# Splitting the stores of the last two chunks into a multiple of 16 rows and a rest, and giving the last two token tiles their own PSUM banks and a second store queue

## Chip, cores, metric

One core of one Trainium2 chip runs the kernel. The metric is the device time of one execution in microseconds; lower is better. Beside the time there is a profile of an execution, whose span (first to last instruction) is about 1.8 us shorter than the time of the same execution.

Engines: PE is TensorE's matmul, ACT is ScalarE, DVE is VectorE, POOL is GpSimd, SP is the sync engine, which here only issues DMAs. A "store" is a DMA from SBUF to the output in HBM.

## The reference

```
X = rfft(x, axis=1);  Y = X * (filt_r + 1j*filt_i);  y = irfft(Y, n=3008)      # x: 8 x 3008 x 256
h = y.reshape(24064, 256) @ w_in                                                # 256 x 2048
g = h + sin(alpha*h)**2 / (alpha + 1e-9)
out = g @ w_out                                                                 # 24064 x 256, fp32
```

## The kernel before

The Fourier part runs interleaved with the two big products. The tokens are worked through in 48 chunks of 512 (some of 384) columns, counted from 0, so that chunk 47 is the last. For each chunk `hidden` computes the 2048 hidden values, and one chunk later `project` multiplies them with `w_out`, 128 tokens (one token tile) at a time. Columns stand in the order (n2, row), with 94 rows to an n2, so 128 consecutive columns hit two or three runs of output tokens, and each run is one store with one 1 KB row of the output per partition.

```python
C, NR, S, B = 256, 94, 3008, 8
chunks = [(pb, c0, 384 if c0 == 2560 else 512) for pb in range(B // 2)
          for c0 in [*range(0, 2561, 512), *range(2944, 2 * S, 512)]]

def project(k, u):
    pb, c0, n = chunks[k]
    t, half = divmod(u, 2)
    if t % 2 == 0 and half == 0:
        pso[k] = ops.tile([128, 2, C], FP32, name=f"po_{k}_{t}", tag="o")   # two tiles in one PSUM bank
    for jb in range(8 * half, 8 * half + 8):
        nc.tensor.matmul(out=pso[k][:, t % 2, :], lhsT=v[k][:, jb, 128 * t:128 * t + 128],
                         rhs=w2[:, jb, :], start=(jb == 0), stop=(jb == 15))
    last = 128 * (t + 1) == n
    if half == 1 and (t % 2 == 1 or last):
        nb = t % 2 + 1
        o = opool.tile([128, 2, C], FP32, name=f"o_{k}_{t}", tag="o")
        nc.scalar.copy(out=o[:, 0:nb, :], in_=pso[k][:, 0:nb, :])
        for i in range(nb):
            store(o[:, i, :], pb, c0 + 128 * (t + 1 - nb + i))

def store(o_blk, pb, col):
    p = 0
    while p < 128:
        odd, rest = divmod(col + p, S)
        n2, row = divmod(rest, NR)
        cnt = min(128 - p, NR - row)
        t0 = (2 * pb + odd) * S + 32 * row + n2
        nc.sync.dma_start(out=bass.AP(tensor=out.tensor, offset=out.offset + t0 * C,
                                      ap=[[32 * C, cnt], [1, C]]),
                          in_=o_blk[p:p + cnt, :])
        p += cnt
# ... (cut: transforms, tables, hidden, the schedule)
```

In the last chunk the four tiles (0 to 3) have stores of 42 and 86 rows; 8, 94 and 26; 68 and 60; 34 and 94. After the last `hidden` there is nothing but `project`, 128 matmuls in a row.

The Fourier part of batch 1 is loaded by POOL from an intermediate in HBM.

```python
def load_t2(self, g):
    self.t2[g] = t2pool.tile([128, 6, C], FP16, name=f"t2_{self.b}_{g}", tag="t2")
    for p in range(2):
        a0 = p * NS + 6 * g
        nc.gpsimd.dma_start(out=self.t2[g][64 * p:64 * p + 64, :, :],
                            in_=self.d1[a0:a0 + 6, :, :].rearrange("s n c -> n s c"))
```

Of the kernel before, what the change touches and what calls it, by code (L numbers as in the profile page):

```python
# [17 lines left out]
B, S, C = 8, 3008, 256  # L18
# [8 lines left out]
def dft_tables():  # L27

    n1, n2 = np.arange(N1), np.arange(N2)
    s, q = np.arange(NS), np.arange(NQ)  # L30
    ph = 2 * np.pi * np.outer(n1, s) / N1
    w = np.stack([np.cos(ph), -np.sin(ph)], 1)
    wf = np.zeros((N1, 2, 2, NS, 2))
    wi = np.zeros((2, NS, 2, N1, 2))
    v = np.stack([2 * np.cos(ph), -2 * np.sin(ph)], 0)
    v[0, :, 0], v[1, :, 0] = 1.0, 0.0
    for h in range(2):
        wf[:, h, :, :, h] = w
        wi[:, :, h, :, h] = v.transpose(0, 2, 1) * (8.0 / S)


    kap = np.where(q[:, None] < 32, s + N1 * q[:, None], s + N1 * (95 - q[:, None]))
    sg = np.where(q < 32, 1.0, -1.0)[:, None]
    th = 2 * np.pi * n2[:, None, None] * kap / S
    c, sn = np.cos(th), np.sin(th)
    d = np.zeros((2, N2, NS, 2, NQ))
    d[0, :, :, 0] = c.transpose(0, 2, 1)
    d[1, :, :, 0] = sn.transpose(0, 2, 1)
    d[0, :, :, 1] = (-sn * sg).transpose(0, 2, 1)
    d[1, :, :, 1] = (c * sg).transpose(0, 2, 1)  # L50
    f16 = np.float16
    wf, wi = wf.reshape(N1 * 2, 2, NS, 2), 2 * wi.reshape(2, NS, 2, NR)
    wf0, wi0 = np.zeros((NR, 2, 2, 32)), np.zeros((2, 2, 32, NR))
    wf0[:, :, :, :NS] = wf.transpose(0, 1, 3, 2)
    wi0[:, :, :NS] = wi.transpose(0, 2, 1, 3)
    return (wf.reshape(NR, NK).astype(f16), wi.reshape(NK, NR).astype(f16),
            d.reshape(128, NS, 128).astype(f16),
            wf0.reshape(NR, 128).astype(f16), wi0.reshape(128, NR).astype(f16))
# [3 lines left out]
def kernel(  # L62
# [9 lines left out]
):  # L72
    nc = tc.nc
    wf_host, wi_host, d_host, wf0_host, wi0_host = dft_tables()
    wf_dram = nc.inline_tensor(wf_host, name="wf_tbl")
    wi_dram = nc.inline_tensor(wi_host, name="wi_tbl")
# [13 lines left out]
    def pool(name, bufs, space=None):  # L90
        kw = {} if space is None else {"space": space}
        return ctx.enter_context(tc.tile_pool(name=name, bufs=bufs, **kw))
# [11 lines left out]
    fps = pool("fps", 2, PSUM)  # L104
    hps = pool("hps", 4, PSUM)
    ops = pool("ops", 2, PSUM)


    wf0_t = cpool.tile([NR, 128], FP16)
    nc.sync.dma_start(out=wf0_t, in_=wf0_dram.ap())  # L110
# [138 lines left out]
                                     lhsT=t4_h[ch // 2][0:NK, n0 % 16 + i, cb * 128:cb * 128 + 128])  # L249
            evac(y[:, cb, self.b % 2, n0:n0 + 4, :], psv, on_act)  # L250


    y = cpool.tile([128, 2, 2, 32, NR], FP16)
    y_cols = y.rearrange("p a b n r -> p a (b n r)")


    warm = cpool.tile([128, 1], FP32)
    nc.vector.memset(warm, 0.0)
# [11 lines left out]
    for g in range(2):  # L270
        for k, filt in enumerate((filt_r, filt_i)):
            for q in range(2):
                off, step = ((12 * g) * C, C) if q == 0 else ((N1 - 12 * g) * C, -C)
                marks["filt", g] = nc.gpsimd.dma_start(
                    out=f_t[k][64 * k + 32 * q:64 * k + 32 * q + 32, 12 * g:12 * g + 12, :],
                    in_=bass.AP(tensor=filt.tensor, offset=filt.offset + off,
                                ap=[[N1 * C, 32], [step, 12], [1, C]]))
# [59 lines left out]
    for i in range(4):  # L337
        turn(t2_0[i // 2][:, :, 32 * (i % 2):32 * (i % 2) + 32], t1_0[:, :, 32 * i:32 * i + 32])
        if i % 2 == 1:
            k = i // 2  # L340
            nc.vector.tensor_copy(out=f_t[k][64 - 64 * k:128 - 64 * k, 0:12, :],
                                  in_=f_t[k][64 * k:64 * k + 64, 0:12, :])
# [37 lines left out]
    for i in range(4):  # L380
        ins = nc.sync.dma_start(out=cos_all[:, i, :], in_=bass.AP(tensor=moe_alpha.tensor,
                                                                  offset=moe_alpha.offset + 512 * i,
                                                                  ap=[[0, 128], [1, 512]]))
# [54 lines left out]
    def weights_out(i):  # L438

        for jb in range(4 * i, 4 * i + 4):  # L440
            if jb in range(8, 16):
                nc.scalar.mul(w2[:, jb, :], w_out32[:, jb, :], rec_t[:, jb:jb + 1])  # L442
            else:
# [3 lines left out]
    chunks = [(pb, c0, 384 if c0 == 2560 else 512) for pb in range(B // 2)  # L447
              for c0 in [*range(0, 2561, 512), *range(2944, 2 * S, 512)]]

    v = {}  # L450
    pso = {}
# [16 lines left out]
    def project(k, u):  # L468

        pb, c0, n = chunks[k]  # L470
        t, half = divmod(u, 2)
        if t % 2 == 0 and half == 0:
            pso[k] = ops.tile([128, 2, C], FP32, name=f"po_{k}_{t}", tag="o")
        for jb in range(8 * half, 8 * half + 8):
            nc.tensor.matmul(out=pso[k][:, t % 2, :], lhsT=v[k][:, jb, 128 * t:128 * t + 128],  # L475
                             rhs=w2[:, jb, :], start=(jb == 0), stop=(jb == 15))
        last = 128 * (t + 1) == n
        if half == 1 and (t % 2 == 1 or last):
            nb = t % 2 + 1
            o = opool.tile([128, 2, C], FP32, name=f"o_{k}_{t}", tag="o")  # L480
            nc.scalar.copy(out=o[:, 0:nb, :], in_=pso[k][:, 0:nb, :])  # L481
            for i in range(nb):
                store(o[:, i, :], pb, c0 + 128 * (t + 1 - nb + i))

    def store(o_blk, pb, col):

        p = 0
        while p < 128:
            odd, rest = divmod(col + p, S)
            n2, row = divmod(rest, NR)  # L490
            cnt = min(128 - p, NR - row)
            t0 = (2 * pb + odd) * S + 32 * row + n2
            nc.sync.dma_start(  # L493
                out=bass.AP(tensor=out.tensor, offset=out.offset + t0 * C,
                            ap=[[32 * C, cnt], [1, C]]),
                in_=o_blk[p:p + cnt, :])
            p += cnt




    pending = []

# [52 lines left out]
    for k in range(len(chunks) + 1):  # L556
        for j in range(8):
            if k < len(chunks):
                hidden(k, 2 * j)
                hidden(k, 2 * j + 1)  # L560
            slot(step)
            if k > 0:
                n_half = 2 * (chunks[k - 1][2] // 128)
                for u in range(n_half * j // 8, n_half * (j + 1) // 8):
                    project(k - 1, u)
            slot(step + 0.5)
            step += 1
# [31 lines left out]
```

## Time and profile before

| | before |
|---|---|
| time, median of 3 runs | 809.29 us (809.09 to 810.32) |
| span of the profiled run | 809.6 us |
| start of the last PSUM copy (= end of the last matmul) | 800.57 us |
| from there to the end of the span, called the tail below | 9.05 us |

The profiled run of before took 811.39 us. It is none of the three timed runs, and longer than each of them.

From the page of the kernel before: the span, the busy time of PE, and the shares of the chain of waits that ended last.

```profile
span 809.6 us, 16470 instructions
...
PE 775.8 (96%) x5815; PEld 535.7 (66%) x5815; DVE 658.4 (81%) x1185; ACT 615.5 (76%) x1206; POOL 76.4 (9%) x116
...
PE 86%; DMA 4%; DVE 2%; ACT 2%; issue 1%; SPq 0%; POOL 0%; ACTq 0%; DVEq 0%
```

TensorE is the limit nearly everywhere, so a change at the very end can gain no more than a part of the tail. The timeline of the end (start, length, engine, line, what; SPq is SP's issuing of DMAs):

```profile
797.69 4.80 SPq L493 DMA_DIRECT2D out_dram<-o  x9
...
800.57 0.58 ACT L481 COPY o<-po 128x512 f32<-128x512 f32 x1 [2.91 <-PE po L475]
```

Compute ends at 801.15, and SP has issued its last store by 802.5; 7.1 us follow. What fills them is in the view of busy times by stretch (stretch, its length, busy time of PE, PEld, DVE, ACT and POOL with the number of instructions, granted clock, mean share of the 16 DMA engines, GB/s):

```profile
802.00:804.00 2.00, 0.00 (x0) 0.00 (x0) 0.00 (x0) 0.00 (x0) 0.00 (x0) 0.75 0.40 90
804.00:806.00 2.00, 0.00 (x0) 0.00 (x0) 0.00 (x0) 0.00 (x0) 0.00 (x0) 0.50 0.14 48
806.00:808.00 2.00, 0.00 (x0) 0.00 (x0) 0.00 (x0) 0.00 (x0) 0.00 (x0) 0.50 0.10 34
```

From 804 us on, about two of 16 engines (0.14 x 16 = 2.2) move 48 GB/s. In the packet records of the trace they are two streams, each with a 1 KB packet every 42.3 ns, the longer of them until 807.6. SP, which waits for all stores before it closes, shows it too (who waits for whom, total us, times, longest):

```profile
SPq L594 <- DMA out_dram<-o: 5.3, 3, 2.7
```

The Trainium skill explains the two streams ("DMA: Bandwidth & Descriptors", section "Why a DMA increments its semaphore by 16 and not by 1"): a DMA issued by SP or ACT uses k engines, the largest k up to 16 that divides its row count, and the lowest-numbered k of the 16. 94 = 2 x 47 and 86 = 2 x 43 have no larger usable divisor, so these stores run on two engines, and always on the same two. This trace agrees: two streams, and the 254 rows that fall on the busier engine from the second half of chunk 46 on take 254 x 42.3 ns = 10.7 us.

### The profile page before, as it was taken

To read this page: it belongs to the slowest core of one execution; us is meant where nothing else is said; L and a number is where in the kernel's file an instruction comes from. 1 tells how busy PE (TensorE), PEld (TensorE's weight loads), DVE (VectorE), ACT (ScalarE), POOL (GpSimd) and SP (SyncE) were. 2 spreads that over 40 slices of the span, in tenths; PEclk is the share of its full clock that TensorE was granted. 3 is DMA by queue.
4 is the path that set the end of the run, shared out by engine and by line. 5 is a ranking of instruction groups with operands and counts; after the bars stand their busy time and mean duration, and the time that the engine had idled before them with its cause. 6 is when DMAs were issued, how large, how long until landed. Compare 5 with 4: busy or idle time off the path is not lost.

```text
span 809.6 us, 16470 instructions
## 1 busy us (share of the span) xinstructions
PE 775.8 (96%) x5815; PEld 535.7 (66%) x5815; DVE 658.4 (81%) x1185; ACT 615.5 (76%) x1206; POOL 76.4 (9%) x116
## 2 busy tenths in 40 slices
PE   4799898999999999999999999999999999999995
PEld 2656565667666776767667766767666776766664
DVE  5878688689977998799977998789977999777771
ACT  5577677778887888788877888788787887677762
POOL 3270100200020000200002000200002000000000
PEclk9799999999999999999999999999999999999998
DMA  9943657555476454845465555654656243411111
GB/s 195 286 95 99 153 124 172 179 125 129 109 200 135 96 122 124 218 94 126 103 189 141 114 118 132 180 135 98 137 151 175 60 103 80 127 39 34 38 46 42
DMA packets 84163, 101.62 MB, mean 126 GB/s; under 512 B 10656, under 2 KB 72112, under 8 KB 84080
## 3 DMA queue, kind: packets, MB, share of 16 engines
q1 hardware_dynamic: 74752, 74.83, 34.2%
q0 software_dynamic: 9120, 25.70, 16.7%
q8 instruction: 45, 0.74, 0.4%
q14 instruction: 38, 0.31, 0.1%
q10 hardware_dynamic: 208, 0.04, 0.0%
HBM read 55.96 MB, written 46.66 MB: 127 GB/s over the span
## 4 chain that ended last, share of the span: by engine, by line
PE 86%; DMA 4%; DVE 2%; ACT 2%; issue 1%; SPq 0%; POOL 0%; ACTq 0%; DVEq 0%
PE po L475 38%; PE ph L460 37%; PE pa L170 3%; PE pd L248 2%; PE pb L190 2%; PE pc L221 2%; DMA t<-d 2%; DMA xs<-xf 1%; DVE v L464 1%; PE pd L245 1%; ACT cos_all L463 1%; DMA t_h<-d 1%; SPq L493 0%; ACT w L442 0%; DVE t_h L330 0%
## 5 line engine op out<-in xcount | busy, mean ns | idle before, releaser
L464 DVE SCALAR_TENSOR_TENSOR v<-cos_all,ph 128x512 f16<-128x512 f32 (+1 forms) x768 | 482.9, 671 | 113.2 <-ACT cos_all L463 107.8
L463 ACT ACTIVATE cos_all<-ph 128x512 f32<-128x512 f32 (+1 forms) x768 | 411.0, 592 | 98.5 <-PE ph L460 96.9
L475 PE MATMUL po<-w,v 128*128 128x256 f16 x3008 | 388.7, 272 | 0.0
L460 PE MATMUL ph<-y,w 128*128 128x512 f16 (+1 forms) x1536 | 386.5, 374 | 1.0 <-DVE v L464 0.5
L475 PEld LDWEIGHTS <-v 128*128 128x128 f16 x3008 | 289.2, 98 | 78.2 <-issue 2.0
L460 PEld LDWEIGHTS <-w 128*128 128x128 f16 x1536 | 147.4, 98 | 104.1 <-issue 2.0
L481 ACT COPY o<-po 128x512 f32<-128x512 f32 x96 | 55.4, 577 | 20.8 <-PE po L475 19.4
L193 ACT CAST xf<-pb 128x512 f16<-128x512 f32 x84 | 49.9, 594 | 19.7 <-PE pb L190 15.8
L182 POOL DMA_DIRECT2D t<-d x56 | 36.4, 671 | 209.7 <-DMA out_dram<-o 187.2
L149 ACT CAST y<-pd 128x376 f16<-128x376 f32 x84 | 40.4, 481 | 12.6 <-PE pd L248 6.9
L149 ACT CAST t_h<-pa 96x512 f16<-96x512 f32 x73 | 42.8, 586 | 9.1 <-PE pa L170 8.9
L130 POOL DMA_DIRECT2D x<-in_x_dram x32 | 17.0, 536 | 302.0 <-PE pc L221 160.8
L248 PEld LDWEIGHTS <-t_h 96*128 96x128 f16 x448 | 31.3, 97 | 19.8 <-DMA t_h<-d 2.0
L170 PE MATMUL pa<-x,wf_t 94*96 94x512 f16 x112 | 42.7, 381 | 1.5 <-ACT y L149 1.2
L149 ACT CAST g<-pc 128x512 f16<-128x512 f32 x58 | 34.4, 594 | 8.6 <-PE pc L221 7.9
L248 PE MATMUL pd<-wi_t,t_h 96*128 96x94 f16 x448 | 37.2, 204 | 1.6 <-DMA t_h<-d 1.6
L210 DVE TENSOR_TENSOR xs<-xs,filt 128x512 f16<-128x512 f16 x84 | 35.1, 418 | 3.9 <-DMA xs<-xf 3.8
L211 DVE TENSOR_TENSOR p<-p,xs 128x512 f16<-128x512 f16 x84 | 35.7, 425 | 2.9
L204 DVE TENSOR_TENSOR p<-xf,filt 128x512 f16<-128x512 f16 x84 | 35.1, 418 | 2.1 <-ACT xf L193 2.1
L190 PE MATMUL pb<-t,d_t 128*128 128x256 f16 x168 | 32.0, 272 | 4.8 <-DMA t<-d 3.7
L221 PE MATMUL pc<-p,e_t 128*128 128x256 f16 x168 | 32.1, 273 | 1.0 <-DVE p L211 0.6
L151 DVE CAST t_h<-pa 96x512 f16<-96x512 f32 x39 | 26.5, 680 | 0.6 <-PE pa L170 0.5
(57 smaller groups left out, 252.2 us busy)
## 6 DMA issues: line engine op xcount, KB each, us to landing
x<-in_x_dram POOLq DMA_DIRECT2D x32, 376.0 KB, 5.1
d<-t_h SPq DMA_DIRECT2D x28, 384.0 KB
t<-d POOLq DMA_DIRECT2D x56, 192.0 KB, 6.5
xs<-xf SPq DMA_DIRECT2D x168, 64.0 KB
d<-g SPq DMA_DIRECT2D x56, 192.0 KB
t_h<-d SPq DMA_DIRECT2D x28, 384.0 KB
out_dram<-o SPq DMA_DIRECT2D x72, 94.0 KB
w_out<-in_moe_w_out_dram SPq DMA_DIRECT2D x1, 2048.0 KB
```

What stands on the lines that cost most here:

```text
L149: marks["act"] = nc.scalar.copy(out=dst, in_=src)
L170: marks["pe"] = nc.tensor.matmul(out=ps[0:NK, :], lhsT=wf_t, rhs=self.x[ch][:, 2 * j:2 * j + 2, :], start=True, stop=True)
L182: nc.gpsimd.dma_start(out=self.t2[g][64 * p:64 * p + 64, :, :], in_=self.d1[a0:a0 + 6, :, :].rearrange("s n c -> n s c"))
L190: nc.tensor.matmul(out=ps[:, i, :], lhsT=d_t[:, s, :], rhs=self.t2[s // 6][:, s % 6, :], start=True, stop=True)
L193: nc.scalar.copy(out=self.xf[u], in_=ps)
L221: nc.tensor.matmul(out=ps[:, i, :], lhsT=e_t[:, 2 * w + i, :], rhs=pt[:, i, :], start=(k == 0), stop=(k == len(pr) - 1))
L248: nc.tensor.matmul(out=psv[:, i, :], rhs=wi_t, start=True, stop=True, lhsT=t4_h[ch // 2][0:NK, n0 % 16 + i, cb * 128:cb * 128 + 128])
L460: nc.tensor.matmul(out=ps[:, 0:n], lhsT=w1[:, cb, jb * 128:jb * 128 + 128], rhs=y_cols[:, cb, c0:c0 + n], start=(cb == 0), stop=(cb == 1))
L463: nc.scalar.activation(out=cs[:, 0:n], in_=ps[:, 0:n], func=AFT.Sin, bias=float(np.pi / 2))
L464: marks["snake"] = nc.vector.scalar_tensor_tensor(out=v[k][:, jb, 0:n], in0=cs[:, 0:n], scalar=-1.0, in1=ps[:, 0:n], op0=ALU.add, op1=ALU. ...
L475: nc.tensor.matmul(out=pso[k][:, t % 2, :], lhsT=v[k][:, jb, 128 * t:128 * t + 128], rhs=w2[:, jb, :], start=(jb == 0), stop=(jb == 15))
L481: nc.scalar.copy(out=o[:, 0:nb, :], in_=pso[k][:, 0:nb, :])
```

## The change

Its intent is to keep the tail's stores off the two engines (runs whose count has only small divisors are split into a multiple of 16 and a rest), to let tile 2's copy and stores start while tile 3 is still multiplied (own PSUM bank for each of the last two tiles), and to spread the issuing of the last stores over two queues.

```diff
-        if t % 2 == 0 and half == 0:
+        final = k == len(chunks) - 1 and t > 1
+        if (t % 2 == 0 or final) and half == 0:
             pso[k] = ops.tile([128, 2, C], FP32, name=f"po_{k}_{t}", tag="o")
 ...
-        if half == 1 and (t % 2 == 1 or last):
-            nb = t % 2 + 1
+        if half == 1 and (t % 2 == 1 or last or final):
+            i0 = t % 2 if final else 0
             o = opool.tile([128, 2, C], FP32, name=f"o_{k}_{t}", tag="o")
-            nc.scalar.copy(out=o[:, 0:nb, :], in_=pso[k][:, 0:nb, :])
-            for i in range(nb):
-                store(o[:, i, :], pb, c0 + 128 * (t + 1 - nb + i))
+            nc.scalar.copy(out=o[:, i0:t % 2 + 1, :], in_=pso[k][:, i0:t % 2 + 1, :])
+            for i in range(i0, t % 2 + 1):
+                store(o[:, i, :], pb, c0 + 128 * (t - t % 2 + i), final, k > len(chunks) - 3)
+
+    def runs(cnt):
+        whole = cnt if max(d for d in range(1, 17) if cnt % d == 0) > 7 else cnt - cnt % 16
+        return [(0, whole), (whole, cnt - whole)] if 0 < whole < cnt else [(0, cnt)]

-    def store(o_blk, pb, col):
+    def store(o_blk, pb, col, final, spread):
         p = 0
+        queues = [nc.sync, nc.scalar] if final else [nc.sync, nc.sync]
         while p < 128:
 ...
-            nc.sync.dma_start(out=..., in_=o_blk[p:p + cnt, :])
+            for i, (r0, rows) in enumerate(runs(cnt) if spread else [(0, cnt)]):
+                queues[i].dma_start(out=..., in_=o_blk[p + r0:p + r0 + rows, :])
             p += cnt
```

(The two addresses are cut; they differ by the offset of the run.) In the last chunk 86 becomes 80 + 6, 94 becomes 80 + 14, 68 becomes 64 + 4 and 34 becomes 32 + 2; 42, 8, 26 and 60 stay.

More of the change, by code (lines that the diff above doesn't have):

```diff
@@ L492, in store @@
             t0 = (2 * pb + odd) * S + 32 * row + n2
-            nc.sync.dma_start(
-                out=bass.AP(tensor=out.tensor, offset=out.offset + t0 * C,
-                            ap=[[32 * C, cnt], [1, C]]),
-                in_=o_blk[p:p + cnt, :])
+            for i, (r0, rows) in enumerate(runs(cnt) if spread else [(0, cnt)]):
+                queues[i].dma_start(
+                    out=bass.AP(tensor=out.tensor, offset=out.offset + (t0 + 32 * r0) * C,
+                                ap=[[32 * C, rows], [1, C]]),
+                    in_=o_blk[p + r0:p + r0 + rows, :])
             p += cnt
```

## The prediction

> **What bounds the kernel now.** The page shows PE busy 96% of the 809.6 us span, at full granted clock; the chain of waits gives PE 86%. The change touches only the end. There the timeline shows the last projection matmuls ending at 800.5 us, the last PSUM copy at 800.57 (0.58 us, 128x512), and four output stores issued by SP from 801.18 to 802.5. The remaining 7.1 us hold no compute: it is DMA and a fixed close. In the packet records of the trace the last store packets start at 807.6, SP's wait on the third and fourth stores ends at 805.98 and 807.97, and the span ends 1.65 us after that.
>
> **Why the stores are late.** The Trainium skill, "DMA: Bandwidth & Descriptors", section on why a DMA increments its semaphore by 16, says a DMA from this queue runs on the largest number of engines up to 16 that divides its row count. The trace agrees: after 805 us packets of 1 KB come as two streams, one each 42.3 ns (48 GB/s between 804 and 806 us in the DMA view). A 94- or 86-row store therefore runs on 2 engines with 47 or 43 rows each, always the same two. Counting the rows that fall on the busiest engine from the stores issued at 794.2 on: 73 (second half of chunk 46), 96 (tiles 0 and 1 of the last chunk), 85 (tiles 2 and 3), together 254 packets x 42.3 ns = 10.7 us. They start about 795.5 to 796.5 and end at 807.2 to 807.6: these two engines are a backlog, and the backlog is the tail.
>
> **What the change does.**
> - Rows split into a multiple of 16 and a rest: 94 becomes 80+14, 86 becomes 80+6, 76 64+12, 68 64+4, 34 32+2. The busiest engine gets about 16, 15 and 16 packets in the three groups instead of 73, 96, 85: under 1 us each, so no backlog.
> - More issues: SP spends 0.36 to 0.40 us per store (787.25 to 788.79 in the timeline). Tiles 0 and 1 need 7 issues instead of 5, from 797.69 to about 800.4; then tile 2's two on SP, to 801.15; then the last tile's two, at about 801.15 and 801.55. So SP's issuing becomes the limit of the tail.
> - Own PSUM banks: tile 2 is copied during tile 3's matmuls, and the last copy has 256 columns. From 577 ns for 512 and 481 for 376 columns I estimate 0.36 us, 0.2 saved, which SP's queue mostly swallows.
> - The rests of the last two tiles go to the ACT queue. The skill (same page, "Issuing engines are not separate DMA queues") says that saves issue time only; here that is three issues, about 1.1 us on SP, and it matters as SP is the limit.
>
> **Sum.** Unqueued stores landed 1.35 to 1.72 us after their issue began (the 787 us group). Last issue 801.55 + 1.65 = 803.2 against 807.97 now; close 1.65: span about 804.8, 4.8 us less. Everything before 794 us, 98% of the span, stays. Timed median 809.29 - 4.8 = 804.5 us, 0.6% faster: inside 2%. Of the 4.8 I give about 4.5 to the row split, 0.3 to banks and second queue.
>
> **Signs.** PE still ends at 800.5; two copies of 128x256; final landing 802.8 to 803.6; no stretch with just two DMA streams of 42 ns; 16-engine stores landing within 1.8 us of issue; close still 1.6 to 1.7 us.
>
> **What would make it wrong.** Stores waiting for a completion semaphore of an earlier store (few are reused in turn), or both queues sharing one descriptor generator, so issues take longer: up to +1 us. Stores finishing faster, or the issue being shorter: -0.7 us. Noise of before was 809.09 to 810.32. A change of 2% would need 16 us, twice the tail.

## The result

| | before | after |
|---|---|---|
| time, median of 4 runs | 809.81 us (809.09 to 810.54) | 805.97 us (805.53 to 806.67) |
| span of the profiled run | 809.6 us | 804.9 us |
| start of the last PSUM copy | 800.57 us | 799.93 us |
| tail | 9.05 us | 4.95 us |

The ratio of times is 0.9953, with a 95% interval of 0.9936 to 0.9971. A ratio is the mean time of one kernel's fast runs over that of the other's of the same rounds, so it is not quite the ratio of the medians quoted here.

The direction came out as predicted, and the change stayed inside 2%, as the prediction said. The time did not: 805.97 lies 1.47 us above the point 804.5, and 0.47 above the 805.5 that the prediction's own risk of "up to +1 us" allows. The 4.1 us that the tail gave are 0.7 short of the 4.8 predicted.

From the page after:

```profile
span 804.9 us, 16484 instructions
...
PE 775.8 (96%) x5815; PEld 535.5 (67%) x5815; DVE 658.4 (82%) x1185; ACT 615.8 (77%) x1207; POOL 76.7 (10%) x116
...
PE 86%; DMA 6%; DVE 3%; ACT 2%; issue 1%; SPq 0%; POOL 0%; DVEq 0%; ACTq 0%; POOLq 0%
```

The timeline of its end:

```profile
797.41 4.41 SPq L497 DMA_DIRECT2D out_dram<-o  x10
...
798.18 0.37 ACT L478 COPY o<-po 128x256 f32<-128x256 f32 x1 [1.16 <-PE po L472]
798.59 0.50 ACTq L497 DMA_DIRECT2D out_dram<-o  x1
799.93 0.37 ACT L478 COPY o<-po 128x256 f32<-128x256 f32 x1 [1.37 <-DMA out_dram<-o]
800.34 0.62 ACTq L497 DMA_DIRECT2D out_dram<-o  x2
```

The two copies are there, 0.37 us each. (The profile names a store as what ended the wait before the last copy. In split_last_two_tiles below, the same wait, 1.4 us, is put down to PE, and the copy does need PE's last matmul.) SP now issues without a break from before tile 2's copy until 801.82, that is 1.5 us after the last copy has ended: it is SP that is late. The busy times by stretch, and SP's waits:

```profile
800.00:802.00 2.00, 0.00 (x0) 0.00 (x0) 0.00 (x0) 0.30 (x1) 0.00 (x0) 0.98 0.37 97
802.00:804.00 2.00, 0.00 (x0) 0.00 (x0) 0.00 (x0) 0.00 (x0) 0.00 (x0) 0.50 0.15 45
```

```profile
SPq L595 <- DMA out_dram<-o: 1.2, 2, 0.7
```

The packets of the last stores come in bursts on all 16 engines and are over by 803; SP's closing wait for stores is 1.2 us, where it was 5.3. The backlog of two engines is gone.

### The profile page after: what moved, and what is told of

It is laid out like the page before. It is cut to its first block, busy times and chain, and to the rows that moved or that the text cites. A ratio compares the mean times of both kernels' runs of the same rounds, so it can differ in the third digit from the quotient of the medians.

```text
span 804.9 us, 16484 instructions
## 1 busy us (share of the span) xinstructions
PE 775.8 (96%) x5815; PEld 535.5 (67%) x5815; DVE 658.4 (82%) x1185; ACT 615.8 (77%) x1207; POOL 76.7 (10%) x116
## 4 chain that ended last, share of the span: by engine, by line
PE 86%; DMA 6%; DVE 3%; ACT 2%; issue 1%; SPq 0%; POOL 0%; DVEq 0%; ACTq 0%; POOLq 0%
PE po L472 37%; PE ph L456 37%; PE pa L168 3%; PE pd L246 2%; PE pb L188 2%; DMA xs<-xf 2%; PE pc L219 2%; DMA t<-d 2%; DVE v L460 1%; PE pd L243 1%; DMA t_h<-d 1%; DMA x<-in_x_dram 1%; PE pc L368 1%; ACT cos_all L459 1%; DMA d<-g 1%
## 5 line engine op out<-in xcount | busy, mean ns | idle before, releaser
L478 ACT COPY o<-po 128x512 f32<-128x512 f32 (+1 forms) x97 | 55.7, 574 | 20.4 <-PE po L472 18.0
```

What stands on the lines that cost most here:

```text
L478: nc.scalar.copy(out=o[:, i0:t % 2 + 1, :], in_=pso[k][:, i0:t % 2 + 1, :])
```

## The experiments

Two measures serve all runs. The tail is the time from the start of the last PSUM copy to the end of the span (the first expectations write 4.97 for after, from the rounded span). The time from the 33rd to the 41st sine activation belongs to split_all, further down. The tail is needed because the rest of the kernel is not equally long each time: in the fourteen profiles the last copy starts anywhere from 796.83 to 802.12 us, though from the 257th to the last of the 768 sine activations all take 481.35 to 481.72 us. The spread arises before that, in what is called the opening below: the 257th activation starts anywhere from 307.68 to 312.98 us, and the first of all already from 43.67 to 46.16. A time, even of five rounds, carries some of it; the tail does not.

| run | tail, us | 33rd to 41st sine, us | time, us | ratio to before (95%) |
|---|---|---|---|---|
| before | 9.05 | 11.4 | 809.81 | |
| after | 4.95 | 11.1 | 805.97 | 0.9953 (0.9936 to 0.9971) |
| after_again | 4.96 | 10.6 | 806.94 | 0.9963 (0.9941 to 0.9985) |
| banks_alone | 9.00 | 11.2 | 809.63 | 0.9988 (0.9976 to 1.0000) |
| split_alone | 6.32 | 12.3 | 808.61 | 0.9968 (0.9952 to 0.9984) |
| one_queue | 5.54 | 11.4 | 807.36 | 0.9958 (0.9944 to 0.9971) |
| rests_on_act | 4.27 | 10.5 | 805.89 | 0.9942 (0.9925 to 0.9958) |
| more_issues | 5.91 | 11.3 | 808.06 | 0.9980 (0.9951 to 1.0009) |
| split_last_two_tiles | 6.88 | 11.2 | 807.98 | 0.9979 (0.9957 to 1.0000) |
| split_last_chunk | 4.61 | 12.0 | 806.50 | 0.9961 (0.9932 to 0.9989) |
| no_64 | 4.63 | 11.2 | 806.92 | 0.9960 (0.9928 to 0.9992) |
| balanced | 3.83 | 11.0 | 805.27 | 0.9946 (0.9932 to 0.9959) |
| split_all | 4.74 | 8.6 | 802.83 | 0.9911 (0.9886 to 0.9935) |
| first_and_last | 3.77 | 8.6 | 802.47 | 0.9901 (0.9880 to 0.9922) |

Times of runs with one round (more_issues, split_last_two_tiles, split_last_chunk, no_64) are medians of two and say little; their tails are what counts. The medians of before in the later rounds were 810.56, 809.22, 809.33 and 810.75 us. All kernels gave the correct result.

### banks_alone and split_alone: the parts of the change

banks_alone keeps the own banks and splits nothing:

```diff
-            for i, (r0, rows) in enumerate(runs(cnt) if spread else [(0, cnt)]):
+            for i, (r0, rows) in enumerate([(0, cnt)]):
```

> Tiles 2 and 3 of the last chunk have own PSUM banks and copies, but no store is split (so all are on SP). Theory A: before the change the tail is the backlog of two DMA engines, whose rows are the same in number here, so tail 8.8 to 9.1 us and time within 0.3 us of before. Rival C (the tail is the late start of the stores): the first two of the last four stores start 1.75 us earlier, so the tail falls to 7.5 to 8.2 us.

The tail was 9.00 us, in A's range. (The median time was 0.93 us below before's in the same rounds, more than A's 0.3; the spread of the opening is larger than that.) The last stores were issued earlier (SP's last issue began 0.68 us after the last copy's start, against 1.59 before), and nothing came of it. The busy times by stretch of this run show the two streams as before, 48 GB/s on about two engines:

```profile
803.00:805.00 2.00, 0.00 (x0) 0.00 (x0) 0.00 (x0) 0.00 (x0) 0.00 (x0) 0.50 0.14 48
805.00:807.00 2.00, 0.00 (x0) 0.00 (x0) 0.00 (x0) 0.00 (x0) 0.00 (x0) 0.50 0.05 18
```

So the tail before was the backlog (theory A), not the late start of the stores (rival C).

split_alone keeps the split, with one bank, one copy and one queue:

```diff
-        final = k == len(chunks) - 1 and t > 1
+        final = False
```

> The rows are split as in the change, but tiles 2 and 3 share one PSUM bank and one copy again, and all stores go out on SP. 'Tail' is the time from the start of the last PSUM copy to the end of the span: 9.04 us before, 4.97 us after. Theory A (after the change the tail is limited by how fast SP issues stores, about 0.4 us each, and no longer by two DMA engines): seven stores wait for one copy, the last is issued about 3.0 us after the copy starts, so tail 6.1 to 6.5 us, time about 2.7 us less than before. Theory B (the prediction's share-out: the row split brings all but 0.3 us, banks and second queue are swallowed): tail about 5.3 us, time about 3.8 us less than before.

The tail was 6.32 us, in A's range and a full microsecond above B's. Its timeline has one copy of two tiles again,

```profile
801.34 0.58 ACT L478 COPY o<-po 128x512 f32<-128x512 f32 x1 [2.91 <-PE po L472]
```

and behind it seven stores in a row on SP, the last begun 3.13 us after the copy's start. The split alone takes 9.05 - 6.32 = 2.73 us off the tail, not the "about 4.5" of the prediction; banks and second queue, worth nothing without the split, are worth 1.37 us on top of it, not 0.3.

### one_queue and rests_on_act: is SP's issuing the new limit?

one_queue gives the rests back to SP; rests_on_act moves the rests of tiles 0 and 1 to ACT as well.

```diff
 # one_queue
-        queues = [nc.sync, nc.scalar] if final else [nc.sync, nc.sync]
+        queues = [nc.sync, nc.sync]
 # rests_on_act
-        queues = [nc.sync, nc.scalar] if final else [nc.sync, nc.sync]
+        queues = [nc.sync, nc.scalar] if final or (pb == B // 2 - 1 and col >= 5504) else [nc.sync, nc.sync]
```

> The whole change, but the rests of the last two tiles are issued by SP like the others, none by ACT. Theory A: SP has three more issues of 0.4 us in its chain after the last two copies, tail 5.6 to 6.0 us against 4.97. Rival D (the two queues share what makes the descriptors, so the second queue gains nothing): tail 4.8 to 5.1 us.

> The whole change, and the two rests of tiles 0 and 1 of the last chunk are issued by ACT too, which is idle there. Theory A: SP comes free 0.75 us earlier and waits for the last copy instead, tail 4.2 to 4.5 us, about 0.6 us less than after. Rival D (shared generation): SP's other issues stretch by as much, tail 4.8 to 5.1 us.

one_queue's tail was 5.54 us, 0.59 more than after; that is a little less than A's 5.6 to 6.0, and clear of D's 5.1. rests_on_act's was 4.27, 0.68 less than after and in A's range. Two stores moved from SP to the other queue in one run, three moved back in the other, and the tail follows both times. The queues do not hinder each other so much that the second is useless, which was rival D. This parts the 1.37 us above: 6.32 - 5.54 = 0.78 for the banks, 5.54 - 4.95 = 0.59 for the second queue.

The Trainium skill ("DMA: Bandwidth & Descriptors", "Issuing engines are not separate DMA queues") says that a second issuing engine only saves the sequencer's time of issuing, "which is usually small relative to the DMA itself". The first half agrees with these runs. For the second half: here an issue takes 0.25 to 0.6 us and a store of after's tail 1.3 to 1.9 us from the start of its issue to its landing, so a chain of four or five issues of about 0.4 us is as long as one store.

### more_issues: adding to the suspected cost

```diff
     def runs(cnt):
+        if cnt in (42, 26, 60):
+            return [(0, cnt - cnt % 16), (cnt - cnt % 16, cnt % 16)]
 ...
-                queues[i].dma_start(
+                (nc.sync if cnt == 60 else queues[i]).dma_start(
```

> The whole change, and three more stores of the last chunk (42, 26 and 60 rows) are split needlessly, both parts issued by SP: the same bytes and nearly the same rows on each engine, three more SP issues in the chain of the tail. Tail = start of the last PSUM copy to the end of the span, 4.95 us after. Theory A (SP's issuing limits the tail): 3 x 0.42 us more, tail 6.0 to 6.4 us. Rival E (the tail after the change is the fixed latency of a store and of the close, behind the last copy): 4.9 to 5.2 us.

The tail was 5.91 us, just under A's range, and far above E's 5.2. The last landing came 1.14 us later after the copy's start than in after (4.38 against 3.24), 0.38 for each added issue. The remainder is the close, which was 1.53 us here and 1.71 after: SP goes through its closing waits in a fixed order, 0.06 us each, and which semaphore the last store has decides how many of them are left to do. (The close is 1.71 us behind semaphore 110 and goes down in these steps to 1.35 behind 117. In split_all and first_and_last it is 0.14 us shorter than this order gives, and no run shows why.)

### split_last_two_tiles and split_last_chunk: how much of the split is needed?

```diff
 # split_last_two_tiles
-    store(o[:, i, :], pb, c0 + 128 * (t - t % 2 + i), final, k > len(chunks) - 3)
+    store(o[:, i, :], pb, c0 + 128 * (t - t % 2 + i), final, final)
 # split_last_chunk
-    store(o[:, i, :], pb, c0 + 128 * (t - t % 2 + i), final, k > len(chunks) - 3)
+    store(o[:, i, :], pb, c0 + 128 * (t - t % 2 + i), final, k > len(chunks) - 2)
```

> The whole change, but only the stores of the last two tiles are split; those of tiles 0 and 1 of the last chunk and of chunk 46 go as before. Theory A (two engines work off rows one after another, 42.3 ns each): 169 rows of the earlier stores stay on them, 15 come from the last two tiles, so they end (254 - 184) x 42.3 ns = 3.0 us sooner than before, tail about 6.0 us (5.7 to 6.3), with a stretch of two streams only. Rival C (only the last stores matter): at most 5.0 us, since SP has two issues fewer than after.

> The whole change, but the stores of chunk 46 are not split. Theory A: their 73 rows on the busiest engine are worked off by about 2 us before the last copy starts, and SP is free by then anyway, so tail 4.8 to 5.1 us, as after. Rival F (the change needs both chunks): tail 5.5 us or more.

split_last_two_tiles missed A's range upwards, with a tail of 6.88 us, and is nearly 2 us above C's at most 5.0. The backlog came back, as A said, but it also turned into something that A had left out. SP's waits in this run, and below them SP's issuing in the view by line (min/median/max ns, first and last start):

```profile
SPq L497 <- DMA out_dram<-o: 3.2, 2, 1.7
```

```profile
L497 SPq DMA_DIRECT2D out_dram<-o x9: 251/322/586, 795.9 to 802.5; - x9
```

Stores use a handful of completion semaphores in turn, eight in this trace, and SP does not issue a store before the earlier store with the same semaphore has landed. The 32-row store had to wait for the 86-row store of tile 0 (landed 800.41 us, issued 800.47), and the 80-row store for the 94-row store of tile 1 (landed 802.51, issued 802.53). So an unsplit store can cost twice at the end: its rows queue on two engines, and the eighth store behind it cannot even be issued until they have landed. In the runs with the whole last chunk split SP waits for earlier stores 0.2 us at most before it issues.

split_last_chunk's tail was 4.61 us, below the 4.8 to 5.1 of A, and its last landing, 3.26 us after the copy's start, is that of after (3.24); the close was 0.36 us shorter for the order of the closing waits. Rival F is out: splitting chunk 46 gains nothing.

### no_64: the term that was mis-sized

In after, SP's chain is 0.5 us longer than the prediction has it. These are three single issues of SP, from three narrow windows of the timeline of after: 64 rows, 60 rows and the last 80 rows.

```profile
799.83 0.47 SPq L497 DMA_DIRECT2D out_dram<-o  x1
...
800.34 0.59 SPq L497 DMA_DIRECT2D out_dram<-o  x1
...
801.40 0.42 SPq L497 DMA_DIRECT2D out_dram<-o  x1
```

Tile 2's two issues take 1.20 us until the next can begin (799.83 to 801.03), not 0.75. The records of before, had they been asked, show it too: its eight 64-row stores take 0.49 to 0.61 us to issue, while most of its 72 stores of 94 rows take 0.24 to 0.28. The edit avoids the 64 rows:

```diff
     def runs(cnt):
+        if cnt == 68:
+            return [(0, 60), (60, 8)]
```

> The whole change, but the store of 68 rows in tile 2 is split 60 + 8 instead of 64 + 4 (SP 60, ACT 8): the number of SP issues is the same, and every engine has at most 4 rows of it as before. In the traces so far SP's issue of 64 rows takes 0.47 to 0.61 us and the issue right after it 0.55 to 0.60, others mostly 0.25 to 0.42. Theory G (it is the 64-row issue that makes the chain 0.5 us longer than predicted): the two issues of tile 2 on SP take 0.75 us together instead of 1.2, tail 4.4 to 4.6 us (4.95 after). Rival H (the issues are slow there because both queues issue at once): tail 4.8 to 5.0 us.

The two issues took 0.87 us until the next began, the last landing came 0.33 us earlier than in after (2.91 against 3.24 us after the copy's start), and the tail was 4.63 us: 0.03 outside G's range and below all of H's. So it is the 64 rows that cost, for most of the half microsecond. Two earlier runs speak against rival H as well: in split_alone and one_queue, where SP issues every store and ACT none, the 64-row store takes 0.47 us too. Why SP needs longer for 64 rows than for 60 or 80 is not shown by any run.

### balanced: what the runs pointed to

Only the last chunk is split, all its rests go to ACT, and the last tile's four stores are dealt out two and two, 80 rows first on SP.

```diff
-        queues = [nc.sync, nc.scalar] if final else [nc.sync, nc.sync]
+        queues = [nc.sync, nc.scalar] if spread else [nc.sync, nc.sync]   # spread: k > len(chunks) - 2
+        made = []                            # the loop collects (queue, token, rows, first row)
 ...
+                q = queues[i]
+                if col == 2 * S - 128 and pb == B // 2 - 1 and p == 0:
+                    q = queues[1 - i]        # of the 34 rows: 32 on ACT, 2 on SP
+        if col == 2 * S - 128 and pb == B // 2 - 1:
+            made = [made[2], made[3], made[0], made[1]]
+        # ... then all of made are issued in this order
```

> Built from what the runs so far point to: only the last chunk's stores are split, all rests of it on the ACT queue, and of the last tile SP issues 80 and then 2 rows, ACT 14 and then 32. Theory A: after the last copy each queue has two issues, the last starts about 0.75 us after the copy's start and lands 1.5 to 1.6 us later, tail 3.8 to 4.1 us, 5.0 to 5.2 us under before. If the two queues hinder each other when both issue, 4.3 us as with the rests on ACT, or more.

The tail was 3.83 us, in A's range. The last issue began 0.84 us after the copy's start and the last landing came at 2.41. Of the 1.12 us under after, 0.83 are this earlier landing. The other 0.30 are the close, 1.41 us against 1.71: the last store to land happens to have a late semaphore in the order of the closing waits. That part is luck and not the better share-out. Measured by the last landing, rests_on_act (2.56) is only 0.15 us behind. The time, 0.9946 of before, cannot be told from that of after (0.9953): 1.1 us of tail is less than what the opening varies.

### split_all, after_again and first_and_last: a gain where none was expected

```diff
 # split_all: 600 store issues instead of 440
-    store(o[:, i, :], pb, c0 + 128 * (t - t % 2 + i), final, k > len(chunks) - 3)
+    store(o[:, i, :], pb, c0 + 128 * (t - t % 2 + i), final, True)
```

> The whole change, and the stores of all 48 chunks are split: 600 store issues instead of 440. Theory A (only the tail feels the stores; before it TensorE is the limit): tail 4.9 to 5.0 us, the time from the 257th to the last sine activation unchanged at 481.4 us within 0.4, time as after within 0.3%. Rival I (SP's extra 60 us of issuing, or the freed two engines, are felt in the body): that stretch changes by over 1 us, up or down.

> The changed kernel itself once more, for its tail and time on another chip. All theories: tail 4.9 to 5.0 us (4.6 if the last store's semaphore is late in the order of the closing waits). Theory A with the run-to-run spread of the opening (up to 2 us in the traces): ratio to before 0.9940 to 0.9960.

after_again confirmed its tail, 4.96 us; its ratio, 0.9963, lies just above the range given.

split_all broke theory A. Its body (481.35 us from the 257th sine on) is as A said. Its tail, 4.74 us, is below A's 4.9 to 5.0 for its shorter close alone (1.51 us against 1.71; the last landing, 3.23 us after the copy's start, is that of after). But the time is 802.83 us in the same rounds in which after took 806.94, and part of the gain sits in one place of the opening. From the 33rd to the 41st sine activation, near 80 us, every other profile up to then took 10.5 to 12.3 us, and this one 8.6. (That is 1.9 to 3.7 us of the 4.1 by which the medians differ; the opening varies by enough for the rest.) PE's first use of batch 1's intermediate falls there. In after it waits (the view of the matmul's line: what ended its idle time, and how often):

```profile
  DMA t<-d: 2.3, 1
```

In before PE has that wait for 2.6 us, among its waits from 70 to 95 us,

```profile
PE pb L190 <- DMA t<-d: 2.6, 1, 2.6
```

and in split_all none. The loads themselves, eight of them issued by POOL from 78.3 us in after and 78.1 in split_all, show why; first after, then split_all:

```profile
L180 POOL DMA_DIRECT2D t<-d x8: 673/684/720, 78.3 to 82.8; - x8
...
DMA to landing us min/median/max: 5.7/7.1/7.2
```

```profile
L180 POOL DMA_DIRECT2D t<-d x8: 673/688/720, 78.1 to 82.7; - x8
...
DMA to landing us min/median/max: 3.3/4.4/5.0
```

The same loads land 2.2 to 2.7 us sooner. Just before them, from 76.5 to 78.3 us, after issues stores of 26, 94, 8, 86 and 42 rows, of which 96 rows fall on the busier of the same two engines, which is 4.1 us of work at 42.3 ns each. In after fourteen of the sixteen completions of the first load arrive by 83.22 us and the last two at 83.92 and 83.97; in split_all all sixteen are there by 81.44. So two of sixteen lag by 0.7 us, which fits the two engines with the backlog. But the other fourteen are late too: the load's first packet, on whichever engine, starts 2.79 us after the issue in after and 1.44 us after it in split_all. This delay of 1.3 us is common to all engines, a backlog on two does not account for it, and its cause is not shown.

The last run puts this to the test: the balanced tail, and splits in the first two chunks only.

```diff
-    ... final, k > len(chunks) - 2)
+    ... final, k < 2 or k == len(chunks) - 1)
 # (cut: the condition of queues, so that the rests of the first two chunks stay on SP)
```

> The balanced tail, and the stores of the first two chunks are split as well (both parts on SP there), no others. In the run with all stores split, TensorE's wait for the first load of batch 1's intermediate (1.9 to 2.6 us in the other runs, 'PE pb waits for DMA t') was gone, and the stretch from the 33rd to the 41st sine activation took 8.6 us against 10.5 to 12.3 in all others. Theory K (rows of the first two chunks' stores, queued on two DMA engines, hold up that load): that stretch is 8.4 to 9.0 us here too, with the wait gone, tail 3.7 to 4.1 us, ratio to before 0.988 to 0.993. Rival J (the gain came from stores of later chunks or from chance): the stretch stays at 10.5 to 12.3 us, ratio as balanced, 0.993 to 0.996.

The stretch took 8.6 us, PE's wait for the load was gone, the tail was 3.77 us, and the ratio 0.9901, all in K's ranges. Its loads:

```profile
L180 POOL DMA_DIRECT2D t<-d x8: 673/688/720, 80.2 to 84.8; - x8
...
DMA to landing us min/median/max: 3.1/4.1/4.7
```

Rival J (later chunks, or chance) falls. The first packet of the load starts 1.43 us after its issue here, as in split_all (1.44), and 2.65 to 2.84 us after it in the twelve profiles without splits in the first chunks. So it is shown that the unsplit stores of the first two chunks hold up this load; that they do so as rows queued on two engines is shown for the smaller part of the delay only. Balanced has the same tail (3.83 us) without these splits; its ratio, 0.9946 (0.9932 to 0.9959), lies clear of this one. This kernel is the fastest: 802.47 us, against 810.75 for before in the same rounds. It has not been timed in the same rounds as after; against before its interval (0.9880 to 0.9922) does not touch that of after (0.9936 to 0.9971).

## Why the prediction was right or wrong

- **The bound and the place of the gain: right.** Matmuls and everything up to the last copy stay; the tail shrinks from 9.05 to 4.95 us.
- **The backlog of two engines: right.** Without the split the tail stays at 9.00 us (banks_alone), and with it the stretch of two 42.3 ns streams is gone.
- **SP's issuing as the next limit: right in kind.** Moving issues off SP and adding some moves the tail by 0.4 us or less each, in the predicted direction (rests_on_act, one_queue, more_issues).
- **The step that failed: "SP spends 0.36 to 0.40 us per store".** That was read from four stores of 84, 44, 50 and 78 rows. In the changed tail there are a 64-row store (0.47 us) and the 60-row store behind it (0.59). "Tile 2's two on SP, to 801.15" is 0.75 us in the prediction and 1.20 us in the trace. The last issue begins 1.47 us after the last copy's start instead of 0.98, its landing takes 1.77 us instead of 1.65, and the close 1.71 instead of 1.65. (The four stores that the prediction names landed 1.62 to 1.72 us after their issue began; its lower figure of 1.35 is not in the trace.) Together the tail is 4.95 us instead of the 4.2 that the prediction's 804.8 implies. The prediction named "issues take longer: up to +1 us" as a risk, of two queues that share a descriptor generator; no_64 shows that the 64 rows did most of it.
- **The share-out: wrong.** "About 4.5 to the row split, 0.3 to banks and second queue" is 2.73 to the split, 0.78 to the banks and 0.59 to the queue, where each is added to the ones before it. If SP is the limit, what starts SP earlier and what takes stores from it count in full; the prediction said that SP would become the limit and then did not count them so.
- **The number: off by more than the failed step.** Of the 1.47 us between 804.5 and 805.97, 0.72 are the tail. Another 0.52 are the starting point: the same kernel before had a median of 809.29 us in three runs and 809.81 with one more. The remaining 0.23 are less than the 1.1 us that separate the runs of after (4.8 us in after_again). The interval of the ratio (0.9936 to 0.9971) includes the predicted 804.5 / 809.29 = 0.9941.
- **"Everything before 794 us stays": right for this change**, but it hid that unsplit stores cost 1.9 to 3.7 us near 80 us (10.5 to 12.3 us for a stretch that takes 8.6 without them), which the change leaves there.

Left open: why a 64-row store takes SP longer to issue, why all engines begin the load near 80 us later behind unsplit stores, what else makes the opening vary by up to 5 us from run to run, and how first_and_last would stand against after in the same rounds.

## What to carry to other kernels

Look at the row counts of stores: a run of rows whose count has only small divisors sits on a few DMA engines. In this kernel such stores were felt at the end and where an urgent load came behind them, but not in between. Once the backlog at the end was split away, the number of issues per queue became the cost; count them with the measured issue time of that very size, and deal them out over the queues. If a change is worth half a percent, measure the stretch that it touches in the profile, because the rest of the kernel varies by as much.

## What the Trainium skill lacked or had wrong

- "DMA: Bandwidth & Descriptors", "Issuing engines are not separate DMA queues": the sequencer's time is called usually small relative to the DMA. Here a store of after's tail took 0.25 to 0.6 us to issue and 1.3 to 1.9 us to land, and the second queue was worth 0.59 us for three stores and 0.68 for two more.
- The same page gives no issue time by row count. In before SP took mostly 0.24 to 0.28 us for 94 rows, 0.37 to 0.42 for 80, and 0.49 to 0.61 for 64.
- The same page, "Why a DMA increments its semaphore by 16 and not by 1", says how k is chosen, but not that stores on few engines delay a load behind them: the same loads landed in 7.1 us (median) behind unsplit stores and in 4.4 behind split ones. About 1.3 us of this is a later first packet on all engines, whose cause is open.
- The same page, "Specifications", gives about 27 GiB/s (29 GB/s) for an engine. Here a lone stream of 1 KB rows into HBM went at 1024 B / 42.3 ns = 24.2 GB/s.
- No page that was used says what the reuse of a few completion semaphores costs: SP waited 3.2 us for two earlier stores before it could issue the last ones (split_last_two_tiles).
